# Attention and two expert layers on one core: another order of the first batch, block-diagonal products in small tiles, and a second plan table

## The chip, the cores and the metric

One core of a Trainium2 chip runs the whole program in one launch. The metric is the device time in microseconds. The kernel before takes 1292.18 us (median of 3 runs, 1291.85 to 1292.27). Engines: PE is TensorE (PEld its weight loads), DVE is VectorE, ACT is ScalarE, POOL is GpSimd, SP is SyncE, which issues most DMAs.

## What is computed

```python
# q, k, v: (8 batches, 8 heads, 576, 64); m = 32 landmarks, each the mean of 18 neighbouring rows
A  = sm(q, k_lm)         # 576 x 32: the softmax of all rows against the landmarks
Bm = sm(q_lm, k_lm)      # 32 x 32
C  = sm(q_lm, k)         # 32 x 576
Z  = Bm.T / (norm1(Bm) * norminf(Bm) + 1e-06)
for _ in range(6): Z = 2 * Z - Z @ Bm @ Z      # iterated inverse
x  = A @ Z @ C @ v                             # per head; then 4608 tokens x 512
h  = x @ w_in; x = max(0.01 * h, h) @ w_out    # 512 -> 2048 -> 512, all tokens
# then a gate picks one of 8 experts per token, and each token runs through
# relu(x @ w1[e]) @ w2[e], 512 -> 1024 -> 512, scaled by the gate's probability
```

## The kernel before

**Layout.** Batches are taken one after the other. Eight heads are two groups (g = 0, 1) of four heads; the four heads of a group stand on partitions 0–31, 32–63, 64–95 and 96–127. The attention of a batch ends in two things: `at`, the softmax A in a high and a low part, and `ub`, the product Z C v w_in, also in two parts, so that `h = at x ub` is the hidden layer. Steps run over the 16 blocks of 128 hidden units of a batch. A step ("m") issues the hidden matmuls of the block two steps ahead (`h_mm`, L545: 12 matmuls of 288 columns, four pauses) and then the output matmuls of its own block (`o_mm`, L590 for batch 0 and L595 for the others: four chunks, one for each 128 tokens, four pauses). Every second batch has four more steps ("x") for the rows over 512 tokens. After all batches come the expert steps ("e").

**Who sets the order.** Instructions are issued in the order of the program; each engine keeps that order. In each pause (a *turn*, eight in a step) the program issues what its plan table has for that time: `PLAN` holds (step position, function) of one batch's attention, begun a batch ahead, `gate_plan` those of the gate. A position of .51 falls behind the first output chunk, .88 behind the last one. In the same turns, 1.5 a turn, stands the conversion of w_in and w_out, which come as 64-bit numbers: per block two ScalarE, two VectorE and one GpSimd instruction (`conv_low`, `conv_abs`, `conv_shift`, `conv_sign`, `conv_add`), 32 blocks in all. `conv_to` forces what a step needs. The first batch's attention has no steps to stand in: the list `FIRST` issues it ahead of step 0; a bare number in it is so many conversion turns.

**Names.** `red` sums landmarks (L272); `sc` are the scores of C and Bm, `c_*`, `et`, `tv` the softmax C and its product with v; `sa` are the scores of A, `a_max` ... `a_lo` the softmax A (the *second softmax*); `b_*` is the softmax Bm; `n_g` forms I − B Bᵀ scaled, `n_k` (i = 0 to 5) is a step of the iteration, `n_y` and `n_w` bring in Bm and C v, and `u_mm` makes ub. `eight` (L279) issues matmuls of 64x32 tiles for all heads.

**A product per head** of 32 x 32 is, before, one 128x128 matmul per group: VectorE spreads the left factor over a block diagonal with a mask (`rbd`, L410, L437, L451, L458), copies or adds the rest (L452, L454, L456), and TensorE multiplies. `u0` (u_mm of batch 0) stands at the end of every even step.

PSUM: `psw` hands out two banks in turn, more in the head (`spare`), one from the expert steps on; a bank is free again when its readers are done.

Of the kernel before, what the change touches and what calls it, by code (L numbers as in the profile page):

```python
# [28 lines left out]
KA = 2  # L29
# [37 lines left out]
def kernel(  # L67
# [57 lines left out]
    m4b = C["mask4"].unsqueeze(1).unsqueeze(3).to_broadcast([128, 2, 4, LM])  # L125
# [42 lines left out]
    XE = 0.2  # L168
    XS = .4
# [216 lines left out]
    def bc4(x):  # L386
        return x.unsqueeze(2).to_broadcast([128, 2, 4, LM])
# [13 lines left out]
    def b_nrm(b):  # L401
        bl, nn = A.pop((b, "bl")), A.pop((b, "nn"))
        bb = A[b, "bb"] = small("bb", [128, 2, 2, LM])
        DVE.tensor_reduce(out=nn[:, 2:4], in_=bl, axis=AX.X, op=ALU.add)
        DVE.tensor_scalar(out=nn[:, 2:4], in0=nn[:, 2:4], scalar1=1e-9, scalar2=None, op0=ALU.add)
        DVE.reciprocal(out=nn[:, 2:4], in_=nn[:, 2:4])
        DVE.tensor_tensor(out=bb[:, 0], in0=bl, in1=bcm(nn[:, 2:4]), op=ALU.mult)
        DVE.transpose(out=bb[:, 1].rearrange("p g m -> p (g m)"), in_=bb[:, 0].rearrange("p g m -> p (g m)"))
        rb = A[b, "rb"] = small("rbd", [128, 2, 4, LM], 2)
        DVE.tensor_tensor(out=rb, in0=bc4(bb[:, 1]), in1=m4b, op=ALU.mult)  # L410

    def n_g(b):
        bb, rb = A[b, "bb"], A.pop((b, "rb"))
        ps = A[b, "gps"] = psw()
        for g in range(2):
            PE.matmul(out=ps[:, g * LM:(g + 1) * LM], lhsT=rb[:, g].rearrange("p h m -> p (h m)"),
                      rhs=bb[:, 1, g, :])
        nn = small("nn2", [128, 2, 2])
        DVE.tensor_reduce(out=nn, in_=bb, axis=AX.X, op=ALU.add)
        nbt = small("rbd", [128, 2, 4, LM], 2)  # L420
# [10 lines left out]
        DVE.tensor_tensor(out=gs, in0=ps[:, :2 * LM].rearrange("p (g m) -> p g m", g=2),  # L431
                          in1=bcm(cc), op=ALU.mult)
# [3 lines left out]
        rb = A[b, "rb"] = small("rbd", [128, 2, 4, LM], 2)  # L436
        DVE.tensor_tensor(out=rb, in0=bc4(rx[:, :, 0, :]), in1=m4b, op=ALU.mult)  # L437
        DVE.tensor_tensor(out=rx[:, :, 1, :], in0=rx[:, :, 0, :], in1=eye, op=ALU.add)

    def n_k(b, i):  # L440
        rx, rb = A[b, "rx"], A[b, "rb"]
        lo, hi = {0: (0, 1), 5: (1, 2)}.get(i, (0, 2))
        ps = psw()
        for g in range(2):
            PE.matmul(out=ps[:, 64 * g + LM * lo:64 * g + LM * hi], lhsT=rb[:, g].rearrange("p h m -> p (h m)"),  # L445
                      rhs=rx[:, g, lo:hi, :])
        p4 = ps[:, :128].rearrange("p (g a m) -> p g a m", g=2, a=2)
# [34 lines left out]
    def u_mm(b, s, n=2):  # L482
# [15 lines left out]

    PLAN = [
# [8 lines left out]
        (8.25, a_exp, 0), (8.3, a_max, 1), (8.4, a_sub, 1), (8.63, n_k, 1), (8.8, a_sum, 0), (8.9, a_exp, 1),
        (9.0, a_mul, 0), (9.26, n_k, 2), (9.4, a_sum, 1), (9.5, a_mul, 1), (9.88, n_k, 3), (10.05, a_tr, 0),
        (10.2, a_hi, 0), (10.3, a_lo, 0), (10.51, n_k, 4), (10.7, a_tr, 1), (10.85, a_hi, 1), (10.95, a_lo, 1),  # L510
        (11.13, n_k, 5), (11.15, wi_load, 0), (11.3, wi_load, 1), (11.63, n_y), (12.13, n_w), (12.63, u_mm, 0),
        (13.88, u_mm, 2), (15.13, u_mm, 4), (18.13, u_mm, 6),
# [531 lines left out]

    grp = ExitStack()
# [64 lines left out]
    for s in range(NSLOT):  # L1110
        t0 = T1 + NF * s
        x = t0 - 1 - XE - 5 * XS
        if s == 0:
            p = t_early + 0.4
        else:
            p = max(t_rest + 0.5 if s == KA else 0, x - 2.5)
        if s == 1:
            p = max(p, T1 - 2)
            x = max(x, p + 1)
        put([(p, part(s_tab, s))])  # L1120
        put([(p + 0.6 if j < XGB else x + XS * (j - XGB) + 0.1, part(s_gather, s, j)) for j in range(5)])
        put([(x + XS * j, part(s_xt, s, j)) for j in range(5)])
# [4 lines left out]
    def first_h(_, t):  # L1127
# [45 lines left out]
    for t in range(TE + 1):  # L1173
# [42 lines left out]
        if t < NFC and t % 2 == 0 and t // 2 + 2 < NS:  # L1216
            u0(t // 2 + 2)
# [74 lines left out]
```

## Time and profile before

| | us |
|---|---|
| median of 3 runs | 1292.18 |
| profiled execution | 1291.29 |
| its span | 1289.5 |
| TensorE busy | 1227.5 (95%) |
| VectorE, ScalarE, GpSimd busy | 609.0, 512.9, 468.8 |
| mean granted clock of TensorE | 0.988 of full speed |

The page's digits show VectorE at 5 to 8 tenths in the first five slices of 32 us and at 3 to 5 after; TensorE at 5, 7, 8, 8 tenths in the first four slices and at 9 or more from the fifth to the last but one. In a timeline a row merges equal instructions that follow each other; its second number runs from the first start to the last end, and since matmuls overlap, a group's share of TensorE is read from its start to the next group's start. A matmul in 32-bit floats stands as two instructions, so "x4" are two matmuls.

### The profile page before, as it was taken

The numbers are of one execution on the slowest core, as the hardware profiler recorded it, in microseconds if no ns is written. First come the engines' busy times: TensorE is split into PE (matmuls) and PEld (weight loads), VectorE is DVE, ScalarE is ACT, GpSimd is POOL, SyncE is SP. The second block draws the span as 40 slices with busy tenths as digits, with TensorE's granted clock in tenths as the row PEclk, the third lists the DMA queues.
The fourth block names the chain that finished last, engine by engine and source line by source line (L and its number), as shares of the span: only waits on it lengthen the run. The fifth ranks groups of instructions, "written<-read, shape, count | busy, mean of one in ns | idle before, by whom it ended". The sixth has DMA issues, their size and how long they took to land.

```text
span 1289.5 us, 22321 instructions
## 1 busy us (share of the span) xinstructions
PE 1227.5 (95%) x8630; PEld 1006.5 (78%) x8630; DVE 609.0 (47%) x1546; ACT 512.9 (40%) x1117; POOL 468.8 (36%) x362
## 2 busy tenths in 40 slices
PE   5788999999999999999999999999999999999994
PEld 2545567877877887878887888789989999999993
DVE  7788566535455435465435443244353332333311
ACT  3455355444344343344343444542343343333211
POOL 1544324433423424423424334624353333333201
PEclk9989999999999999999999999999999999999997
DMA  7677462351151241151141122341454334433001
GB/s 254 232 246 238 147 233 60 115 166 53 34 190 52 66 166 52 36 188 52 67 165 52 41 92 90 120 139 34 156 175 157 122 103 140 131 120 109 21 31 39
DMA packets 61891, 151.04 MB, mean 117 GB/s; under 512 B 10192, under 2 KB 19664, under 8 KB 61776
## 3 DMA queue, kind: packets, MB, share of 16 engines
q1 hardware_dynamic: 54736, 130.61, 30.8%
q0 software_dynamic: 7040, 18.92, 4.5%
q8 instruction: 70, 1.15, 0.4%
q14 instruction: 45, 0.37, 0.1%
HBM read 121.87 MB, written 27.63 MB: 116 GB/s over the span
## 4 chain that ended last, share of the span: by engine, by line
PE 79%; DVE 9%; issue 4%; ACT 1%; DMA 0%; POOL 0%; POOLq 0%; SPq 0%; DVEq 0%; ACTq 0%
PE acc L595 34%; PE hps L899 14%; PE hps L545 14%; PE psw L279 3%; PE acc L604 3%; PE psw L921 2%; PE acc L590 2%; PE psw L445 1%; PE psw L867 1%; PE psw L634 1%; DVE kT L272 1%; DVE qlm L272 1%; PE psw L378 1%; DVE te L199 1%; PE psw L642 1%
## 5 line engine op out<-in xcount | busy, mean ns | idle before, releaser
L595 PE MATMUL acc<-wo,gh 128*128 128x512 f32 x1216 | 383.8, 397 | 0.0
L562 POOL TENSOR_TENSOR gl<-hs,gh 128x512 fp32r<-128x512 f32 x112 | 147.1, 1313 | 311.5 <-ACT gh L561 183.2
L595 PEld LDWEIGHTS acc<-wo,gh 128*128 128x128 f32 x1216 | 217.6, 188 | 48.2 <-issue 11.7
L545 PE MATMUL hps<-at,ub 128*128 128x288 f32 x1536 | 253.4, 307 | 1.6 <-DVE hs L551 1.5
L545 PEld LDWEIGHTS hps<-at,ub 128*128 128x128 f32 x1536 | 220.9, 191 | 33.7 <-issue 20.0
L595 PE MATMUL acc<-wo,gl 128*128 128x512 f32 x608 | 238.0, 391 | 0.0
L551 DVE TENSOR_TENSOR hs<-hps,hs 128x288 f32<-128x288 f32 x224 | 98.9, 451 | 130.0 <-ACT hs L549 129.8
L908 DVE SCALAR_TENSOR_TENSOR gl<-hps,gh 128x288 fp32r<-128x288 f32 (+1 forms) x128 | 54.0, 423 | 197.3 <-ACT gh L904 197.3
L595 PEld LDWEIGHTS acc<-wo,gl 128*128 128x128 f32 x608 | 114.2, 188 | 25.0
L549 ACT ACTIVATE hs<-hps 128x288 f32<-128x288 f32 x256 | 101.9, 414 | 74.3 <-PE hps L545 71.1
L904 ACT ACTIVATE gh<-hps 128x288 fp32r<-128x288 f32 x128 | 52.8, 412 | 176.1 <-PE hps L899 111.6
L561 ACT CAST gh<-hs 128x512 fp32r<-128x512 f32 x112 | 69.5, 620 | 119.0 <-PE acc L595 94.4
L855 POOL DMA_INDIRECT xg<-x_d,gi x40 | 41.6, 1041 | 132.4 <-DVE gi L847 61.1
L940 POOL DMA_INDIRECT out_dram<-rows,gi x40 | 40.6, 1015 | 124.8 <-DVE rows L938 75.8
L492 DVE TENSOR_TENSOR ub<-psw,ub 128x512 fp32r<-128x512 f32 (+1 forms) x70 | 41.3, 632 | 70.0 <-ACT ub L491 70.0
L899 PE MATMUL hps<-xt,wo 128*128 128x288 f32 x480 | 68.7, 297 | 0.0
L899 PE MATMUL hps<-at,wo 128*128 128x288 f32 x480 | 68.0, 296 | 0.0
L899 PEld LDWEIGHTS hps<-xt,wo 128*128 128x128 f32 x480 | 66.4, 188 | 1.6
L899 PEld LDWEIGHTS hps<-at,wo 128*128 128x128 f32 x480 | 65.8, 188 | 1.6
L491 ACT CAST ub<-psw 128x512 fp32r<-128x512 f32 (+1 forms) x70 | 34.6, 547 | 65.6 <-PE psw L279 65.6
L595 PE MATMUL acc<-ub,gh 128*128 128x512 f32 x192 | 59.8, 393 | 0.0
L887 POOL TENSOR_TENSOR wo<-wraw,wo 128x1024 fp32r<-128x1024 f32 x20 | 48.0, 2398 | 23.3 <-ACT wo L883 23.0
(244 smaller groups left out, 1805.0 us busy)
## 6 DMA issues: line engine op xcount, KB each, us to landing
wraw<-in_moe_w_dram SPq DMA_DIRECT2D x64, 512.0 KB, 4.1
wi<-wi_d SPq DMA_DIRECT2D x56, 512.0 KB, 4.5
kT<-in_k_dram SPq DMA_DIRECT2D x32, 288.0 KB, 5.1
qT<-in_q_dram SPq DMA_DIRECT2D x32, 288.0 KB, 5.3
raw<-in_moe_w_in_dram SPq DMA_DIRECT2D x16, 512.0 KB, 5.2
vraw<-in_v_dram SPq DMA_DIRECT2D x16, 512.0 KB, 5.4
raw<-in_moe_w_out_dram SPq DMA_DIRECT2D x16, 512.0 KB, 4.6
x_d<-rows SPq DMA_DIRECT2D x32, 256.0 KB, 3.3
```

Of the source, the lines that this page charges most:

```text
L492: DVE.tensor_sub(out=u[:, :, 1, :], in0=p3, in1=u[:, :, 0, :].bitcast(F32))
L545: PE.matmul(out=ps[:, :HT], lhsT=us[:, wl, c:c + 128], rhs=at[:, al, 2 * (b % 2) + g, c0:c1], start=(n == 0), stop=(n == 5))
L549: ACT.mul(out=hs[:, c0:c1], in_=ps[:, :HT], mul=0.01)
L551: DVE.tensor_max(out=dst[:, c0:m], in0=ps[:, :m - c0], in1=hs[:, c0:m])
L561: ACT.copy(out=gh[:, :512], in_=src)
L562: POOL.tensor_tensor(out=gl, in0=src, in1=gh[:, :512].bitcast(F32), op=ALU.subtract)
L595: PE.matmul(out=acc(key, j), lhsT=g[hl][:, j * 128:(j + 1) * 128], rhs=wsel[:, wl, :], start=(f == 0 and i == 0), stop=(f == nf - 1 and i ...
L855: POOL.indirect_dma_start(out=xg[:n, :], out_offset=None, in_=x2_d[0:rows, :], in_offset=IND(ap=M[s, "gi"][:n, 0, j:j + 1], axis=0), bound ...
L887: (POOL if n % 2 else DVE).tensor_tensor(out=r[:, :, 1], in0=raw.rearrange("p (f c) -> p f c", f=2), in1=r[:, :, 0].bitcast(F32), op=ALU.s ...
L899: PE.matmul(out=ps[:, :HT], lhsT=wr[:, wl, d * 128:(d + 1) * 128], rhs=xt[:, al, d, c0:c1], start=(n == 0), stop=(n == 11))
L904: ACT.activation(out=gh[:, c0:c1], in_=ps[:, :HT], func=AF.Relu)
L908: DVE.scalar_tensor_tensor(out=lo, in0=ps[:, a - c0:b - c0], scalar=0.0, in1=gh[:, a:b].bitcast(F32), op0=ALU.max, op1=ALU.subtract)
```

## The change

- `diag` is new: a product per head is four matmuls of 32x32 tiles on the diagonal. `n_g`, `n_k` and `n_y` use it; the spread copies `rbd` go. An `n_k` adds its old value with a second set of `diag` products against the identity, into the same bank, and one ScalarE copy hands the result to the next `n_k`, where three VectorE instructions did.
- `FIRST` has another order: the second softmax (`sa`, `a_max`, ...) stands ahead of and between the iteration, 21 conversion turns instead of 30. The first batch's scores of A lie in `hs`.
- `u0` of batch 0 moves from the end of an even step to position .51 of the odd step behind it.
- `PLAN` has other positions, mostly .51 and .88, and batch 1 has a table of its own, `PLAN_1`. `gate_plan` moves the gate's later parts behind. The transposes of the expert steps (`s_xt`) get other positions.

```diff
-                A[b, "st", g] = wide("st")[:, :S]
+                A[b, "st", g] = (wide("st")[:, :S] if b else gp.tile([128, S], F32, name="hs", tag="hs", bufs=2))
...
+    def diag(out, lhs, rhs, start=True, stop=True):
+
+        for p in range(4):
+            h = slice(32 * p, 32 * p + 32)
+            PE.matmul(out=out[h], lhsT=lhs[h], rhs=rhs[h], start=start, stop=stop, skip_group_check=True)
...
-        rb = A[b, "rb"] = small("rbd", [128, 2, 4, LM], 2)
-        DVE.tensor_tensor(out=rb, in0=bc4(bb[:, 1]), in1=m4b, op=ALU.mult)
...
     def n_k(b, i):
-        rx, rb = A[b, "rx"], A[b, "rb"]
+
+        rx = A[b, "rx"]
         lo, hi = {0: (0, 1), 5: (1, 2)}.get(i, (0, 2))
         ps = psw()
         for g in range(2):
-            PE.matmul(out=ps[:, 64 * g + LM * lo:64 * g + LM * hi], lhsT=rb[:, g].rearrange("p h m -> p (h m)"),
-                      rhs=rx[:, g, lo:hi, :])
...
-        if i < 5:
-            DVE.tensor_tensor(out=nb, in0=bc4(p4[:, :, 0, :]), in1=m4b, op=ALU.mult)
-            DVE.tensor_copy(out=nx[:, :, 0, :], in_=p4[:, :, 0, :])
-        if i > 0:
-            DVE.tensor_tensor(out=nx[:, :, 1, :], in0=p4[:, :, 1, :], in1=rx[:, :, 1, :], op=ALU.add)
...
+            c, m, e = 64 * g + LM * lo, 64 * g + LM, 64 * g + 2 * LM
+            diag(ps[:, c:c + LM * (hi - lo)], rx[:, g, 0, :], rx[:, g, lo:hi, :], stop=hi == 1)
+            diag(ps[:, m:e], C["eye"], rx[:, g, 1, :], start=hi == 1)
+        nx = A[b, "rx"] = small("rx", [128, 2, 2, LM], 2)
+        ACT.copy(out=nx[:, :, lo:, :], in_=ps[:, :128].rearrange("p (g a m) -> p g a m", g=2, a=2)[:, :, lo:, :])
...
-        (3.625, sc, 1), (4.125, sc, 0), (4.0, b_max), (4.3, c_max, 0), (4.5, c_max, 1), (4.52, b_exp),
+        (3.88, sc, 1), (4.2, b_max), (4.4, b_exp), (4.88, sc, 0), (5.05, c_max, 0), (5.15, c_exp, 0), (5.2, c_max, 1),
...
+        (2.88, sc, 1), (3.2, b_max), (3.4, b_exp), (4.51, sc, 0), (4.7, c_max, 0), (4.8, c_exp, 0), (4.9, c_max, 1),
...
-        P += [(t, g_l2), (t + 0.1, g_l3), (2.88 + NX * (b % 2), g_l4), (3.4 + NX * (b % 2), g_sc)]
+        P += [(t, g_l2), (t + 0.1, g_l3), (3.51 + NX * (b % 2), g_l4), (4.0 + NX * (b % 2), g_sc)]
...
+    put([(2 * i - 2.49, part(u0, i)) for i in range(2, NS)])
...
-        x = t0 - 1 - XE - 5 * XS
+        xp = [t0 + x for x in (-3.45, -3.08, -2.45, -2.08, -1.45)]
...
-        (c_max, 0), (b_nrm,), (c_exp, 0), (n_g,), (c_max, 1), 6, (et, 0, 0), (c_exp, 1), (et, 0, 1), 4,
-        (n_k, 0), (c_rec, 0), (tv, 0), (et, 1, 0), 4, (et, 1, 1), (n_k, 1), (v_load, 1), (sa, 0), (sa, 1), 2,
+        (sa, 0), 2, (c_max, 0), (b_nrm,), (c_exp, 0), (n_g,), (sa, 1), (a_max, 0), (a_sub, 0), (c_max, 1),
+        (et, 0, 0), (et, 0, 1), (c_exp, 1), (a_max, 1), (a_sub, 1), (n_k, 0), (a_exp, 0), (c_rec, 0), (tv, 0),
...
-        if t < NFC and t % 2 == 0 and t // 2 + 2 < NS:
-            u0(t // 2 + 2)
```

Three places in the order of the engines. First VectorE in the head of before, between the second and the third `n_k` (`te` are conversions, `rbd` and `rx` the iteration, `tn` and `csm` the softmax C):

```order
L452 COPY rx<-acc_237 128x2x32
L456 COPY rx<-rx 128x2x32
L355 TENSOR_SCALAR csm<-csm 128x1
L356 RECIPROCAL csm<-csm 128x1
L383 TENSOR_SCALAR tn<-acc_247,csm 128x64
L199 TENSOR_SCALAR te<-te 128x512
L203 SCALAR_TENSOR_TENSOR te<-raw,te 128x512
L451 TENSOR_TENSOR rbd<-psw_287,cst 128x256
L452 COPY rx<-psw_287 128x2x32
L454 TENSOR_TENSOR rx<-psw_287,rx 128x2x32
```

In the changed kernel the hand-over stands on ScalarE (`raw` and `te` are conversions, `hs` the exponential of the second softmax, `et` copies of the softmax C):

```order
L348 ACTIVATE sc,csm<-sc,csm 128x576
L445 COPY rx<-psw_257 128x128
L303 ACTIVATE hs<-hs 128x576
L445 COPY rx<-hps 128x128
L192 ACTIVATE raw<-raw 128x512
L188 ACTIVATE te<-raw 128x512
L363 COPY et<-acc_332 128x512
L366 COPY et<-acc_338 64x128
L445 COPY rx<-acc_346 128x128
```

The iteration's results moved from VectorE to ScalarE, where they stand between exponentials, conversions and copies.

Second, VectorE in a steady batch of before, ahead of `sc` 1 (`pay`, `grk`, `gpf`, `gpi` are the gate's last part, `kT` and `qlm` the landmark sums, the last of which `sc` 1 waits for):

```order
L272 TENSOR_REDUCE qlm<-qT 128x32
L702 TENSOR_REDUCE pay<-gex 128x5
L703 TENSOR_SCALAR pay<-pay 128x5
L704 RECIPROCAL pay<-pay 128x5
L705 TENSOR_SCALAR pay<-cst 128x5
L706 TENSOR_TENSOR grk<-psw_5254,cst 128x40
L708 TENSOR_TENSOR grk<-grk,oh 128x40
L709 TENSOR_REDUCE gpf<-grk 128x5
L710 CAST gpi<-gpf 128x5
L272 TENSOR_REDUCE kT<-kT 128x32
L551 TENSOR_TENSOR hs<-hps,hs 128x288
L272 TENSOR_REDUCE qlm<-qT 128x32
```

And the same place of the changed kernel:

```order
L269 TENSOR_REDUCE kT<-kT 128x32
L553 TENSOR_TENSOR hs<-hps,hs 128x288
L269 TENSOR_REDUCE qlm<-qT 128x32
L553 TENSOR_TENSOR hs<-hps,hs 128x288
L704 TENSOR_REDUCE pay<-gex 128x5
L705 TENSOR_SCALAR pay<-pay 128x5
L706 RECIPROCAL pay<-pay 128x5
L707 TENSOR_SCALAR pay<-cst 128x5
L708 TENSOR_TENSOR grk<-psw_5658,cst 128x40
L710 TENSOR_TENSOR grk<-grk,oh 128x40
L711 TENSOR_REDUCE gpf<-grk 128x5
L712 CAST gpi<-gpf 128x5
```

The gate's eight instructions moved from ahead of the last two landmark sums to behind them.

Third, TensorE around one full `n_k` of batch 2 before:

```order
L595 MATMUL acc_1690<-wo_2173,gl 128x512
L445 MATMUL psw_2434<-rx,rbd 128x64 x2
L595 MATMUL acc_1696<-wo_2173,gh 128x512 x2
L595 MATMUL acc_1696<-wo_2173,gl 128x512
L595 MATMUL acc_1705<-wo_2173,gh 128x512 x2
```

And in the changed kernel:

```order
L597 MATMUL acc_1827<-wo_2297,gl 128x512
L387 MATMUL psw_2607<-rx 32x64 x4
L387 MATMUL psw_2607<-rx,cst 32x32 x4
L387 MATMUL psw_2607<-rx 32x64 x4
L387 MATMUL psw_2607<-rx,cst 32x32 x4
L597 MATMUL acc_1846<-wo_2297,gh 128x512 x2
```

Two matmuls over the whole array became sixteen over 32x32 tiles, at the same kind of place behind the first output chunk.

## Rows read from the trace of the kernel before

**Rows 1.** Busy time by stage: stretch, length, then each engine's busy us; PEclk.
```profile
53.95:173.15 119.20, 108.48 (x713) 62.53 (x711) 86.57 (x195) 58.38 (x129) 45.66 (x35) 0.96 0.68 223
289.50:764.00 474.50, 470.29 (x3779) 380.47 (x3778) 239.03 (x669) 200.99 (x499) 173.67 (x141) 1.00 0.27 89
```

**Rows 2.** Timeline of TensorE in the head: start us, us, engine line op.
```profile
16.78 1.06 PE L416 MATMUL psw<-bb,rbd 128*128 128x32 f32 x4 [2.99 <-DVE rbd L410]
...
44.60 1.11 PE L279 MATMUL acc<-wi,wt 64*32 64x256 f32 x16 [0.47 <-DVE wt L480]
...
46.49 7.62 PE L545 MATMUL hps<-at,ub 128*128 128x288 f32 x36
```

**Rows 3.** Timeline of the other engines in the head.
```profile
21.36 0.24 ACT L369 COPY et<-hps 64x128 f32<-64x128 f32 x1
...
27.57 0.48 DVE L290 STREAM_TRANSPOSE st<-psw 128x288 f32<-128x288 f32 x1 [0.19 <-PE hps L279]
...
41.23 1.40 POOL L326 TENSOR_TENSOR at<-s,at 128x576 fp32r<-128x576 f32 x1 [2.80 <-ACT at L322]
...
49.02 1.30 POOL L216 TENSOR_TENSOR wi<-raw,te 128x512 uint32<-128x512 uint32 x1
```

**Rows 4.** Timeline of TensorE in steps 4 to 7: the two longest waits.
```profile
89.68 1.12 PE L365 MATMUL psw<-cst,sc 128*128 128x128 f32 x4 [3.48 <-DVE ub L492]
...
107.43 0.93 PE L279 MATMUL psw<-wi,wt 64*32 64x256 f32 x16 [2.52 <-DVE st L290]
```

**Rows 5.** Groups of VectorE: line, operation, count | busy us, mean ns.
```profile
L451 DVE TENSOR_TENSOR rbd<-psw,cst 128x256 f32<-128x256 f32 x37 | 15.5, 419 | 11.8 <-PE psw L445 11.8
...
L456 DVE COPY rx<-rx 128x64 f32<-128x64 f32 x8 | 2.4, 299 | 0.0
```

**Rows 6.** The chain that ended last: one step's four output chunks of batch 0.
```profile
154.93 3.43 PE acc L590 x8
```

**Rows 7.** Timeline of TensorE: `sc` 1 of two batches.
```profile
487.98 0.76 PE L279 MATMUL psw<-kT,qlm 64*32 64x320 f32 x12
489.32 0.73 PE L279 MATMUL psw<-kT,qlm 64*32 64x320 f32 x4 [0.58 <-DVE qlm L272]
...
577.93 0.76 PE L279 MATMUL psw<-kT,qlm 64*32 64x320 f32 x12
579.92 0.73 PE L279 MATMUL psw<-kT,qlm 64*32 64x320 f32 x4 [1.23 <-DVE qlm L272]
```

**Rows 8.** Timeline of VectorE: the gate's last part, and the sum behind it.
```profile
485.15 0.19 DVE L702 TENSOR_REDUCE pay<-gex 128x5 f32<-128x40 f32 x1
...
487.50 0.75 DVE L272 TENSOR_REDUCE kT<-kT 128x32 f32<-128x576 f32 x1
```

**Rows 9.** Timeline of TensorE: one full `n_k` between output chunks.
```profile
518.33 0.55 PE L445 MATMUL psw<-rx,rbd 128*128 128x64 f32 x4
518.69 0.71 PE L595 MATMUL acc<-wo,gh 128*128 128x512 f32 x2
```

**Rows 10.** Timeline of TensorE: blocks in small tiles, and output matmuls around one.
```profile
500.95 0.90 PE L378 MATMUL psw<-vraw,et 128*32 128x64 f32 x40
...
506.49 0.62 PE L595 MATMUL acc<-wo,gh 128*128 128x512 f32 x2
506.94 0.39 PE L595 MATMUL acc<-wo,gl 128*128 128x512 f32 x1
507.26 0.71 PE L279 MATMUL psw<-qT,kT 64*32 64x288 f32 x16
507.91 0.73 PE L595 MATMUL acc<-wo,gh 128*128 128x512 f32 x2
...
539.05 1.09 PE L279 MATMUL psw<-wi,wt 64*32 64x256 f32 x32
```

**Rows 11.** Timeline of ScalarE and of TensorE at the end of the attention.
```profile
827.35 1.99 ACT L883 CAST wo<-wraw 128x1024 fp32r<-128x1024 f32 x2
...
831.13 0.66 PE L634 MATMUL psw<-cst,rows 128*128 128x128 f32 x4 [2.04 <-DVE xt L870]
```

More of the change, by code (lines that the diff above doesn't have):

```diff
@@ L408, in b_nrm @@
         DVE.transpose(out=bb[:, 1].rearrange("p g m -> p (g m)"), in_=bb[:, 0].rearrange("p g m -> p (g m)"))
[L409 to L410 removed]
     def n_g(b):
[L413 to L414 removed]
+        bb = A[b, "bb"]
+        ps = psw()
         for g in range(2):
[L416 to L417 removed]
+            diag(ps[:, 64 * g:64 * g + LM], bb[:, 1, g, :], bb[:, 1, g, :])
         nn = small("nn2", [128, 2, 2])
         DVE.tensor_reduce(out=nn, in_=bb, axis=AX.X, op=ALU.add)
[L420 removed]
+        nbt = small("nbt", [128, 2, 4, LM])
         nb, nt = nbt[:, 0], nbt[:, 1]
@@ L430, in n_g @@
         gs = small("bl", [128, 2, LM])
[L431 removed]
+        DVE.tensor_tensor(out=gs, in0=ps[:, :128].rearrange("p (g m) -> p g m", g=2)[:, :, :LM],
                           in1=bcm(cc), op=ALU.mult)
@@ L508 @@
[L508 to L512, printed above, removed]
+        (3.88, sc, 1), (4.2, b_max), (4.4, b_exp), (4.88, sc, 0), (5.05, c_max, 0), (5.15, c_exp, 0), (5.2, c_max, 1),
@@ new lines @@
+        (5.3, b_nrm), (5.4, c_exp, 1), (5.6, c_rec, 0), (5.88, et, 0, 0), (5.89, et, 0, 1),
+        (6.51, tv, 0), (6.52, et, 1, 0), (6.55, v_load, 1), (6.7, c_rec, 1), (6.88, et, 1, 1), (6.89, n_g),
+        (7.51, sa, 0), (8.51, sa, 1), (8.7, a_max, 0), (8.75, a_sub, 0), (8.88, tv, 1), (8.89, n_k, 0),
+        (9.1, a_exp, 0), (9.15, a_max, 1), (9.25, a_sub, 1), (9.51, n_k, 1), (9.6, a_sum, 0), (9.7, a_exp, 1),
+        (9.8, a_mul, 0), (9.88, n_k, 2), (10.1, a_sum, 1), (10.2, a_mul, 1), (10.51, n_k, 3), (10.6, a_tr, 0),
@@ new lines @@
+        (10.88, n_k, 4), (10.9, a_hi, 0), (11.0, a_lo, 0), (11.15, wi_load, 0), (11.2, a_tr, 1), (11.3, wi_load, 1),
+        (11.51, n_k, 5), (11.6, a_hi, 1), (11.7, a_lo, 1), (11.88, n_y), (12.51, n_w), (12.88, u_mm, 0),
+        (13.88, u_mm, 2), (14.88, u_mm, 4), (18.51, u_mm, 6),
+    ]
+    PLAN_1 = [
+        (0.05, qk_load, 'k', 0), (0.1, qk_load, 'q', 0), (0.15, qk_load, 'k', 1), (0.2, qk_load, 'q', 1),
+        (0.3, qk_load, 'k', 2), (0.4, qk_load, 'q', 2), (0.5, qk_load, 'k', 3), (0.6, qk_load, 'q', 3),
+        (0.7, red, 'k', 0), (0.9, red, 'q', 0), (1.0, v_load, 0), (1.15, red, 'k', 1), (1.4, red, 'q', 1),
+        (1.65, red, 'k', 2), (1.9, red, 'q', 2), (2.15, red, 'k', 3), (2.4, red, 'q', 3),
+        (2.88, sc, 1), (3.2, b_max), (3.4, b_exp), (4.51, sc, 0), (4.7, c_max, 0), (4.8, c_exp, 0), (4.9, c_max, 1),
+        (5.1, b_nrm), (5.2, c_exp, 1), (5.4, c_rec, 0), (5.88, et, 0, 0), (5.89, et, 0, 1),
+        (6.51, tv, 0), (6.52, et, 1, 0), (6.55, v_load, 1), (6.7, c_rec, 1), (6.88, et, 1, 1), (6.89, n_g),
+        (7.88, sa, 0), (8.51, sa, 1), (8.7, a_max, 0), (8.75, a_sub, 0), (8.88, tv, 1), (8.89, n_k, 0),
+        (9.1, a_exp, 0), (9.15, a_max, 1), (9.25, a_sub, 1), (9.6, a_sum, 0), (9.7, a_exp, 1), (9.8, a_mul, 0),
+        (9.88, n_k, 1), (10.1, a_sum, 1), (10.2, a_mul, 1), (10.51, n_k, 2), (10.6, a_tr, 0), (10.88, n_k, 3),
+        (10.9, a_hi, 0), (11.0, a_lo, 0), (11.15, wi_load, 0), (11.2, a_tr, 1), (11.3, wi_load, 1),
+        (11.6, a_hi, 1), (11.7, a_lo, 1), (11.88, n_k, 4), (12.3, n_k, 5), (12.51, n_y), (12.88, n_w),
+        (13.51, u_mm, 0), (14.51, u_mm, 2), (15.51, u_mm, 4), (18.51, u_mm, 6),
@@ L523, in attn_plan @@
         return [(start(b - 1) + pos if pos < NFC else start(b) + pos - NFC, part(fn, b, *a))
-                for pos, fn, *a in PLAN]
+                for pos, fn, *a in (PLAN_1 if b == 1 else PLAN)]
     G = {}
@@ L1115 @@
         else:
-            p = max(t_rest + 0.5 if s == KA else 0, x - 2.5)
+            p = max(t_rest + 0.5 if s == KA else 0, xp[0] - 2.5)
         if s == 1:
             p = max(p, T1 - 2)
-            x = max(x, p + 1)
+            xp = [max(x, p + 1 + i / 100) for i, x in enumerate(xp)]
         put([(p, part(s_tab, s))])
-        put([(p + 0.6 if j < XGB else x + XS * (j - XGB) + 0.1, part(s_gather, s, j)) for j in range(5)])
-        put([(x + XS * j, part(s_xt, s, j)) for j in range(5)])
+        put([(p + 0.6 if j < XGB else xp[j - XGB] + 0.1, part(s_gather, s, j)) for j in range(5)])
+        put([(xp[j], part(s_xt, s, j)) for j in range(5)])
     def first_u0(_, s):
```

45 lines of the change are left out of this document (12 added, 33 removed).

## The prediction

> **What bounds the kernel now.** I read the busy time by stage first, then TensorE's timeline in each stage, then VectorE's and ScalarE's where TensorE waits. The reader is to see three stages. From 289.5 to 764 us, most of the steady run of batches 2 to 7, TensorE is busy 470.3 of 474.5 us [rows 1]: every instruction put on TensorE there makes the kernel longer, and beside that only a wait of TensorE is worth removing. Before 46.5 us TensorE follows the first batch's attention, with VectorE between its groups [rows 2, 3]. In steps 0 to 15 (53.95 to 173.15 us) it is busy 108.5 of 119.2 us, so 10.7 are idle, and its mean granted clock is 0.96, which loses 0.04 x 119.2 = 4.8 more [rows 1]. The two longest waits there, 3.48 + 2.52 = 6.0 us, end on VectorE [rows 4].
>
> The sum is made against the profiled execution: 1291.29 us, of which the span is 1289.5; the median of the runs is 1292.18, 0.9 us more.
>
> **A. The head up to the first hidden-layer matmul.** Before, that matmul starts at 46.49 us, 29.7 us behind the n_g matmuls of 16.78 [rows 2]. In the new order the first half of the second softmax's scores stands ahead of n_g: a score half, two transposes of 0.48 [rows 3] and a maximum come before the normalisation, while a masked copy goes, so n_g starts about 1.2 us later, and n_k 0, behind another score half and five transposes, near 21.7 us. From there VectorE is out of the iteration. One n_k is then a TensorE group of about 1.0 us (n_g's four instructions took 1.06 [rows 2]), a ScalarE copy of 0.25 (0.24 for 64x128 [rows 3]) and two hand-overs of 0.1, 1.45 in all, 8.7 for six. In between stand one tv of some 1.4, one et of 1.3, and on ScalarE an exponential that ends near 24.1 and two conversion pairs: n_k 5 ends near 32.6, n_y near 33.4, n_w near 35, and u_mm 0 starts near 35.3 instead of 44.60 [rows 2], 9.3 earlier. The stage does not end there: u_mm 1 needs the fourth converted block, and GpSimd reaches it late. The low half of the last attention rows, 1.40, can start near 35.4, and two conversion additions of 1.30 stand behind it [rows 3]: 39.4, with some stretching 40. The two u_mm took 1.89 (44.60 to 46.49), so one takes 0.95, and the first hidden matmul starts near 41. I take −5.5. Bounds: −9.3 if those additions come early, 0 if ScalarE's conversions stand ahead of the copies as VectorE's did. Nine fewer conversion turns stand in the head (21 for 30); seven of them are forced before step 0 ends its first part, under 36 hidden matmuls, which hide them.
>
> **B. Steps 0 to 15.** VectorE loses seven groups of instructions, in all 48.2 us over eight batches; the largest and the smallest are shown [rows 5]. That is 6.0 us less for batch 1. ScalarE gets six copies of 0.25, 1.5 us. Batch 1's reductions and first scores come up to a step earlier, and a u_mm of the first batch stands alone in each odd step. I let the waits for VectorE shrink by the 6.0 us of work that goes, and the loss of clock that follows such waits by 3.5 of its 4.8: −9.5. Against it stand 1.4 us for batch 1's iteration on TensorE (D): −8.1, say −8. What is late next is u_mm: its result has three o_mm chunks until its reader, three quarters of 3.43 us [rows 6], 2.6 us, where it had a whole step. Bounds: −14 (all 15.5 of idle time and clock, less 1.4), and +4 if each of six u_mm holds its reader 0.7 us longer than TensorE waits now.
>
> **C. The scores of batches 2 to 7.** sc 1 stands after the second o_mm chunk of step 3, and its last four instructions wait for the last reduction: 489.32 against 487.98, and 579.92 against 577.93 [rows 7]. Delays of 1.34 and 1.99 alternate by the batch's parity, six in all: 3 x 1.34 + 3 x 1.99 = 10.0. On VectorE eight gate instructions stand ahead of the last two reductions, from 485.15 to 487.50 [rows 8]. The new plan puts the gate (3.51) behind them and sc 1 two chunks later (3.88): the reductions are done 2.3 us earlier and asked for 1.4 us later, 3.7 against delays of up to 2.0. I take −10.0; the upper bound is −6, if 0.7 stays in each.
>
> **D. The iteration on TensorE, batches 2 to 7.** Before, an n_k is four 128x128 instructions: 0.36 us to the next start, and the o_mm pair behind it takes 0.71 [rows 9] where an undisturbed pair takes 0.62 [rows 10]: 0.45 in all. Now it is sixteen 32x32 matmuls, four rounds of four, each matmul two instructions. What a block in small tiles costs is read from two: sixteen instructions of 288 columns, two rounds, take 0.71 us, thirty-two of 256 columns, four rounds, 1.09 [rows 10]. The difference, 0.38 us over 1024 − 576 columns, is 0.85 ns a column. Of the 0.65 us from 507.26 to the next start that leaves 0.16; with 0.09 ahead of the block (506.94 to 507.26 is 0.32, undisturbed starts are 0.23 apart) and 0.11 behind it (0.73 for 0.62), a block costs 0.35 beside its columns [rows 10]. No row shows four row groups, so the rounds are bounded: 54 ns for 64 columns, 27 to 54 for 32. A full n_k is 4 x 54 + 4 x (27 to 54) = 0.33 to 0.43, with 0.35 some 0.73: +0.28. n_k 5, eight short rounds, +0.23; n_k 0 the same, less the 0.26 of entry and exit that it shares with tv, −0.03; n_g and n_y, four short rounds, +0.06 each. Per batch 4 x 0.28 + 0.32 = 1.44 (0.9 to 2.0); six batches +8.6 (5.4 to 11.8). ScalarE's copy is due three chunks or more later, so no wait is added. The Trainium skill says that changing the tiling mode drains TensorE (TensorEngine Tiling (Array Packing), Tiling Modes); the trace agrees, with those 0.09 us, which n_k did not pay before.
>
> **E. The end of the attention.** At 831.13 TensorE has waited 2.04 us for a bank; ScalarE did two weight casts from 827.35 on, 1.99 us, ahead of the copy that frees it [rows 11]. That transpose now stands a chunk earlier, ahead of those casts. The wait should fall to about 0.5: −1.5, and with some clock behind it −2 (−4 to +1, since three transposes now stand in one place).
>
> **Sum.** −5.5 − 8 − 10 + 8.6 − 2 = −16.9; 1291.3 − 16.9 + 0.9 = 1275. The likeliest case's own range is 1267 to 1284.
>
> **Rivals.**
> *Four row groups take turns (slower).* The sixteen matmuls of an n_k write one bank. If they go one after the other, a full n_k streams 16 x 54 + 16 x (27 to 54) ns, 1.3 to 1.7 us instead of 0.33 to 0.43, and a batch costs 7 to 9 us more instead of 1.4; over seven batches 49 to 63 instead of 10, so 1314 to 1328, say 1320. It decides from 3.9 us a batch on, where the other terms (25.5, and 1.4 in B) are used up. For it: every row group in this trace writes a bank of its own. Against it: tv's forty instructions of 64 columns, in four column groups of one bank, take 0.90 us [rows 10] where 40 x 54 ns would be 2.2; here too each tile has partitions of its own. The Trainium skill states that different row tiles cannot access the same PSUM bank simultaneously (TensorEngine Tiling (Array Packing), Restrictions and Gotchas); no run here shows it, and by that rule the time is this rival's.
> *VectorE stays late.* For it: at 89.68 its subtraction came 3.48 us late [rows 4], and u_mm's reader is now half a step away, so the wait moves there. Against it: 6 us less work. A and B give nothing, and 1.4 is added: −10 + 8.6 − 2 + 1.4 = −2, 1290.
> *ScalarE holds the iteration.* Conversions, exponentials and copies share one queue; then the second softmax is beside the iteration in name only, and A is 0: 1281. Against it: between the six copies stand only two conversion pairs.
> *All of it goes.* A −8, B −13, D +6: 1265.
>
> **How the numbers follow.** Forecast 0.62, row groups in turn 0.10, VectorE late 0.10, ScalarE 0.10, all of it 0.08. The range 1263 to 1291 leaves out the first rival and the tails. A measurement tells about 0.2%, 2.6 us, from no change, so "same" is 1289.6 to 1294.8: faster 0.62 + 0.10 + 0.08 and half of the VectorE rival, 0.85; same 0.05; slower 0.10.
>
> **What would show it.** A: the first hidden matmul near 41 us, and n_k after n_k with only a copy between them. B: no wait over 2 us between 48 and 160 us and a clock near 1.00. C: the sixteen instructions of sc 1 start together. D: 0.7 us from n_k's first start to the next group's; 1.5 or more means the first rival. E: no wait of 2 us before the last steps. A first hidden matmul later than 46, a u_mm reader that waits over 2 us, or n_k above 1.2 us make the prediction wrong.

## The result, and the profile after

The changed kernel takes 1275.31 us (median of 4 runs, 1274.8 to 1276.42) beside 1292.22 for the kernel before: a ratio of 0.9865, 95% interval 0.9848 to 0.9883. The forecast was 1275. The profiled execution took 1276.42 us with a span of 1274.6, 14.9 less than before: it is the longest of its four, and that of before, 1291.29, lies below every timed run of before, so the traces show 2 us less gain than the medians.

Busy time by stage after the change. Columns as in [rows 1]; the two stretches answer to the two there (steps 0 to 15, and 474.5 us of the steady run):

```profile
49.98:156.90 106.92, 103.17 (x894) 56.92 (x895) 87.17 (x178) 59.96 (x133) 47.16 (x36) 1.00 0.77 255
274.50:749.00 474.50, 470.82 (x4713) 366.67 (x4698) 219.38 (x567) 204.19 (x524) 171.76 (x140) 1.00 0.27 89
```

Steps 0 to 15 are 12.3 us shorter. TensorE is idle 3.75 us there instead of 10.7, and its clock is 1.00 instead of 0.96. The steady run looks as busy as before, which hides that the same work now takes longer there.

To see that, I follow three starts of TensorE through the traces: the first hidden matmul, the `x_mm` of batch 1 and the `x_mm` of batch 7. They cut the span into the head, the first batches, and the attention of batches 3 to 7. Four kernels stand in the table, two of them experiments told below:

| us | head, to first hidden matmul | to `x_mm` of batch 1 | to `x_mm` of batch 7 | span |
|---|---|---|---|---|
| before | 46.49 | 215.94 | 560.19 | 1289.5 |
| tiles alone | 41.30 | 215.84 | 567.84 | 1291.5 |
| order alone | 47.05 | 208.55 | 559.45 | 1278.7 |
| both: the change | 41.27 | 206.14 | 563.65 | 1274.6 |

The head gained 5.2, the first batches 9.8; the run of batches 3 to 7 lost 3.5. From the last hidden matmul of the attention to the first of the experts it is 23.21 us for 25.54, a gain of 2.3; from there to the end 448.7 us for 449.7, a gain of 1.0.

The third column has a spread of its own: four more kernels below, with the same plan for these batches as the change, took 561.2 to 563.6 us (experiments 7, 9, 10 and 12), where the same waits come out longer or shorter (5.1 us in all in the change, 3.2 in experiment 9). So causes in that stretch are read from waits by name, not from its length alone.

The head, on TensorE's timeline (start us, us, engine line op), answers to [rows 2]:

```profile
35.35 1.11 PE L276 MATMUL acc<-wi,wt 64*32 64x256 f32 x16 [0.48 <-DVE wt L464]
38.83 1.08 PE L276 MATMUL psw<-wi,wt 64*32 64x256 f32 x8 [2.37 <-POOL wi L213]
40.26 1.08 PE L276 MATMUL psw<-wi,wt 64*32 64x256 f32 x8 [0.35 <-POOL wi L213]
41.27 7.62 PE L547 MATMUL hps<-at,ub 128*128 128x288 f32 x36
```

`u_mm` 0 starts 9.25 us earlier, and `u_mm` 1 then waits for GpSimd's conversions, as the working of A had it.

The same timeline in the steady run: `sc` 1, which answers to [rows 7], and a full `n_k`, which answers to [rows 9]. The sixteen score instructions now start in one run; the `n_k` takes 0.48 us from its first start to the next group's.

```profile
475.38 0.77 PE L276 MATMUL psw<-kT,qlm 64*32 64x320 f32 x16
...
507.43 0.39 PE L597 MATMUL acc<-wo,gl 128*128 128x512 f32 x1
507.75 0.31 PE L387 MATMUL psw<-rx 32*32 32x64 f32 x8
507.88 0.24 PE L387 MATMUL psw<-rx,cst 32*32 32x32 f32 x8
507.94 0.29 PE L387 MATMUL psw<-rx 32*32 32x64 f32 x8
508.06 0.24 PE L387 MATMUL psw<-rx,cst 32*32 32x32 f32 x8
508.23 0.73 PE L597 MATMUL acc<-wo,gh 128*128 128x512 f32 x2
```

What TensorE still waits for: the longest wait of steps 4 to 7, which answers to [rows 4], and then the waits from batch 1's `x_mm` to batch 7's (waiter and what released it: us in total, times, longest):

```profile
87.52 0.66 PE L362 MATMUL psw<-cst,sc 128*128 128x128 f32 x4 [2.21 <-DVE ub L476]
```

```profile
PE hps L547 <- DVE csm L352: 2.1, 3, 0.7
PE hps L547 <- DVE hs L553: 1.5, 1, 1.5
PE psw L276 <- DMA wi<-wi_d: 1.4, 2, 0.7
```

The 1.5 us were there before. The two other lines are new, and no term of the prediction had them: a hidden matmul that waits for VectorE in batches 3, 5 and 7, and `u_mm` waiting for its weights' DMA. At the end of the attention the longest wait left is one of an expert transpose for ScalarE, where 2.04 us stood before [rows 11]:

```profile
819.76 0.66 PE L869 MATMUL psw<-cst,xg 128*128 128x128 f32 x4 [0.61 <-ACT xt L637]
```

### The profile page after: what moved, and what is told of

It is laid out like the page before. It is cut to its first block, busy times and chain, and to the rows that moved or that the text cites. A ratio compares the mean times of both kernels' runs of the same rounds, so it can differ in the third digit from the quotient of the medians.

```text
span 1274.6 us, 25205 instructions
## 1 busy us (share of the span) xinstructions
PE 1224.5 (96%) x10166; PEld 981.4 (77%) x10166; DVE 583.0 (46%) x1394; ACT 522.0 (41%) x1165; POOL 472.1 (37%) x362
## 4 chain that ended last, share of the span: by engine, by line
PE 82%; DVE 6%; issue 5%; DMA 2%; ACT 1%; POOL 0%; ACTq 0%; POOLq 0%
PE acc L597 35%; PE hps L547 15%; PE hps L901 14%; PE psw L276 4%; PE acc L606 3%; PE acc L592 2%; PE psw L923 2%; DMA wi<-wi_d 2%; PE psw L387 2%; PE psw L869 1%; PE psw L636 1%; DVE te L196 1%; PE psw L375 1%; DVE te L200 1%; PE psw L644 1%
## 5 line engine op out<-in xcount | busy, mean ns | idle before, releaser
L547 PE MATMUL hps<-at,ub 128*128 128x288 f32 x1536 | 239.9, 304 | 4.7 <-DVE csm L352 2.3
L547 PEld LDWEIGHTS hps<-at,ub 128*128 128x128 f32 x1536 | 212.3, 189 | 30.9 <-issue 17.1
L889 POOL TENSOR_TENSOR wo<-wraw,wo 128x1024 fp32r<-128x1024 f32 x20 | 51.1, 2557 | 31.2 <-ACT wo L885 30.9
```

The source lines that it names most:

```text
L547: PE.matmul(out=ps[:, :HT], lhsT=us[:, wl, c:c + 128], rhs=at[:, al, 2 * (b % 2) + g, c0:c1], start=(n == 0), stop=(n == 5))
L889: (POOL if n % 2 else DVE).tensor_tensor(out=r[:, :, 1], in0=raw.rearrange("p (f c) -> p f c", f=2), in1=r[:, :, 0].bitcast(F32), op=ALU.s ...
```

## Experiments

The runs were made on several chips, on which the kernel before took 1290.1 to 1292.2 us, so kernels are compared by ratio to it, or by the stretches of their traces.

**1 and 2. The tiles alone, the order alone.** The first is the kernel before with `diag` and the changed `b_nrm`, `n_g`, `n_k`, `n_y`; the second is the changed kernel with those functions as before. In short, for both:

```diff
 (kernel before)                       (kernel after)
-def bc4 / masked copies in n_*        -def diag
+def diag, n_* in 32x32 tiles          +def bc4 / masked copies in n_*
```

> The kernel before with the diagonal tiles alone (diag, and b_nrm, n_g, n_k, n_y as changed), all places as before. Theory: TensorE pays 1.0 us a batch from batch 2 and about that in batch 1 (+7), the eight sc waits stay (they hang on VectorE's reductions), and the waits for the four-fold copies go in the head and in steps 0 to 15 (the four that the trace of before puts down to rbd: 8.6 us in all, some of it given to other waits): 1287 to 1295. Rival: the gain of the change is VectorE's relief, wherever the work stands: 1282 or less.

> The changed kernel with the iteration as before (four-fold copies on VectorE, whole 128-row matmuls): the new order alone. Theory: TensorE saves the 7 us of the tiles, the sc waits stay gone, and VectorE's extra work (0.5 us or more an iteration step) comes back as waits where the plan is dense, the head and steps 0 to 15, 7 us or more: 1273 to 1283, and no better than the change. Rival: the order does all of it: 1268 or less.

Measured: tiles alone 1293.83 us, ratio 1.0011 (1.0001 to 1.0022); order alone 1282.29, ratio 0.9922 (0.9903 to 0.9941). Both theories hold in the total, and the table above says where each acts; not in the place, since the tiles alone give 0.1 us in the first batches, where the first theory saw part of its gain. The head is the tiles' work alone: 41.30 with the old list. The first batches are the order's: 7.4 us without the tiles, 9.8 with them, while the tiles without the order give 0.1. In the steady run the tiles cost 7.65 us without the order, and the order alone gives 0.7, far less than the 7.8 that its score blocks save (24.83 to 17.05 us for the twenty score blocks there); new waits take most of the rest, above all that of experiment 4 (1.3 us in each of three batches there). Of the tiles' 7.65 us, D's blocks explain some 5.

**3. A later `u_mm` 2.**

```diff
-(13.88, u_mm, 2), (14.88, u_mm, 4)
+(14.51, u_mm, 2), (15.88, u_mm, 4)
```

> The changed kernel with two numbers of the plan for batches 2 to 7 other: u_mm 2 at 14.51 instead of 13.88, u_mm 4 at 15.88 instead of 14.88. Theory: the second u_mm of a batch stands one step behind the first (before: 1.25 steps), and its half of the input weights lands 0.7 to 0.9 us late; with more room the blocks that last 2.0 to 2.2 us fall to 1.22, five of them, so 3 us: 1272.3. Rival: the load is started by the u_mm in front of it and SyncE's queue, so a later u_mm 2 only moves the wait to u_mm 4, and the time stays at 1275.3.

Measured: 1272.63 us, ratio 0.9854 (0.9839 to 0.9869). The waits for the DMA are gone. What a block costs is counted here from the matmul ahead of it to behind the pair that follows it, less what those matmuls take undisturbed: so counted, the twenty-one blocks of `u_mm` from batch 1's `x_mm` to batch 7's cost 25.66 us for 27.91, and 25.65 before the change. The stretch is 2.5 us shorter. The total alone would not show it, for its interval overlaps the change's; but every kernel here with the change's places of `u_mm` has such a wait in that stretch, 0.2 to 1.4 us in all, and none with the later places. One block of `u_mm`, first in the changed kernel, then in this one; what was cut in two by a wait runs through:

```profile
428.99 0.66 PE L276 MATMUL psw<-wi,wt 64*32 64x256 f32 x16
430.40 0.67 PE L276 MATMUL psw<-wi,wt 64*32 64x256 f32 x16 [0.75 <-DMA wi<-wi_d]
```

```profile
430.08 1.09 PE L276 MATMUL psw<-wi,wt 64*32 64x256 f32 x32
```

**4. A later `b_nrm`, and 5. `b_nrm` without L405.** Experiment 5 leaves out the addition of 1e-9 to a sum of exponentials of which one is 1.

```diff
-(5.3, b_nrm), (5.4, c_exp, 1), (5.6, c_rec, 0),
+(5.4, c_exp, 1), (5.6, c_rec, 0), (5.61, b_nrm),
```
```diff
-DVE.tensor_scalar(out=nn[:, 2:4], in0=nn[:, 2:4], scalar1=1e-9, scalar2=None, op0=ALU.add)
```

> The changed kernel with b_nrm of batches 2 to 7 at 5.61, behind c_rec, instead of 5.3. Theory: VectorE's 128x2 addition of L405 stood 1.9 us in batches 3, 5 and 7 because it began while GpSimd worked, and ended within 0.04 us of GpSimd's TENSOR_TENSOR; the accumulation behind it came late, and TensorE stood 0.95 us in each of the three. Half a turn later GpSimd is idle: L405 takes 0.17 us, and 2.9 us go: 1272.4. Rival: another instruction of VectorE takes the wait in its place (c_rec's L352 starts in the same stretch), and the time stays at 1275.3.

> The changed kernel without L405, the addition of 1e-9 to a sum of exponentials. Theory: what holds VectorE is that its operands come through what GpSimd uses at that moment, so the next instruction of that kind, L407 with two operands, stands the 1.7 us instead, TensorE's 0.95 us stays, and the time stays within 0.5 us of 1274.6 (the span). Rival: the stretch belongs to L405's form alone, and its going takes 2.9 us: a span near 1271.7.

Measured: with the later `b_nrm` 1272.07 us, ratio 0.985 (0.9835 to 0.9865), again not clear of the change's interval; without L405 1274.22 in a single run, a span of 1272.3 on a chip where the kernel before was 1.5 us faster, so that figure alone decides nothing. The timelines show why. In the changed kernel an addition of two numbers a partition takes 1.91 us. It begins 0.41 us into an instruction of GpSimd's scatter of the gate (`g_sc`, which the change moved too, from 3.4 to 4.0), stands through the rest of it and through the TENSOR_TENSOR behind it, and ends at 293.16, 0.03 after that; the hidden matmul behind it waits:

```profile
290.84 0.97 POOL L722 DMA_INDIRECT tab_d<-pay,gpi  x1 [0.31 <-issue]
...
291.25 1.91 DVE L405 TENSOR_SCALAR nn<-nn 128x2 f32<-128x2 f32 x1
...
291.83 1.30 POOL L564 TENSOR_TENSOR gl<-hs,gh 128x512 fp32r<-128x512 f32 x1
...
294.30 1.06 PE L547 MATMUL hps<-at,ub 128*128 128x288 f32 x6 [0.70 <-DVE csm L352]
```

Without L405 the product behind it (L406 in that kernel's numbers) stands instead, to 292.45, 0.10 after GpSimd's end:

```profile
290.40 0.17 DVE L405 RECIPROCAL nn<-nn 128x2 f32<-128x2 f32 x1
290.61 1.84 DVE L406 TENSOR_TENSOR bb<-bl,nn 128x64 f32<-128x64 f32 x1
...
291.05 1.30 POOL L563 TENSOR_TENSOR gl<-hs,gh 128x512 fp32r<-128x512 f32 x1
```

So the stall changes its owner, as the theory had it, but TensorE's share of it halves, 0.86 to 0.45 us in each of the three batches (counted from start to start; the theory had it stay): behind the held product only the transpose is left, while behind L405 a reciprocal and the product had to follow first. The kernels of experiments 9 and 10 show the same with L405 in place: in these three batches it began 0.24 to 0.27 us into the scatter's instruction and took 0.17 us, the product behind it stood 1.71 to 1.73 us, and TensorE waited 0.3. So the halving does not need L405 to go, only another moment. With the later `b_nrm` L405 still ends with GpSimd, but loses 0.3 us instead of 1.7, and no matmul waits:

```profile
291.41 0.14 DVE L352 TENSOR_SCALAR csm<-csm 128x1 f32<-128x1 f32 x1
...
291.90 0.46 DVE L405 TENSOR_SCALAR nn<-nn 128x2 f32<-128x2 f32 x1
...
291.01 1.31 POOL L564 TENSOR_TENSOR gl<-hs,gh 128x512 fp32r<-128x512 f32 x1
...
291.77 1.84 PE L547 MATMUL hps<-at,ub 128*128 128x288 f32 x12
```

**6. Both places later**, `u_mm` and `b_nrm`, the two edits above together.

> Both edits of the two kernels beside it. Theory: two waits that don't touch each other, 3 + 2.9 us: 1269.4. Rival: one cover for the other (the batch's weight loads shift with the stretch), so the sum is that of one: 1272.

Measured: 1269.35 us, ratio 0.9827 (0.9814 to 0.9841), the first clear of the change's interval. From batch 1's `x_mm` to batch 7's it takes 558.70 us, 4.95 less than the change and 1.5 less than before. TensorE's idle time in the steady 474.5 us goes from 3.7 to 0.1:

```profile
272.40:746.90 474.50, 474.38 (x4775) 370.62 (x4760) 218.50 (x580) 207.81 (x530) 172.89 (x141) 1.00 0.27 89
```

**7. The old head in the changed kernel, and 8. in the kernel with both later places.**

```diff
-FIRST = [..., (sa, 0), 2, (c_max, 0), (b_nrm,), (c_exp, 0), (n_g,), (sa, 1), ...
+FIRST = [..., (c_max, 0), (b_nrm,), (c_exp, 0), (n_g,), (c_max, 1), 6, ...  (list of before)
```

> The changed kernel with the FIRST list of before, and its second softmax in the wide tile as before. Theory: the head is on the path alone; the first hidden matmul falls back to between 44 and 46.5 us (the iteration now on ScalarE's side keeps some of the gain), all behind it keeps its length: 1278.5 to 1280.5. Rival: the iteration in small tiles is what makes the head short, and the list does nothing: 1275 to 1276.

> Both later places (b_nrm, u_mm of batches 2 to 7) with the head's list of before. Theory: the list of the head gives nothing, since with the tiles alone the first hidden matmul starts at 41.3 already; the time is that of both edits, 0.9827 of before, within 0.0005. Rival: the old list is better by 1 to 2 us, as the single run of each on one chip looked (1274.06 against 1276.04 for the changed list with n_k's matmuls in another order): 0.9815.

Measured: 1274.06 us, ratio 0.9855 (0.9833 to 0.9877), and 1267.74, ratio 0.9826 (0.9813 to 0.9839). In the first the theory fell: the first hidden matmul stays at 41.77 us, so the list does next to nothing. In the second its theory holds: both lists are equal. TensorE's timeline in two more heads: the old list with the tiles (experiment 1), then the new list without them (experiment 2).

```profile
39.41 1.11 PE L279 MATMUL acc<-wi,wt 64*32 64x256 f32 x16 [0.48 <-DVE wt L467]
40.23 1.14 PE L279 MATMUL psw<-wi,wt 64*32 64x256 f32 x16
41.30 2.53 PE L532 MATMUL hps<-at,ub 128*128 128x288 f32 x12
```

```profile
41.13 1.11 PE L277 MATMUL acc<-wi,wt 64*32 64x256 f32 x16 [0.47 <-DVE wt L478]
44.60 1.08 PE L277 MATMUL psw<-wi,wt 64*32 64x256 f32 x8 [2.37 <-POOL wi L214]
46.03 1.08 PE L277 MATMUL psw<-wi,wt 64*32 64x256 f32 x8 [0.35 <-POOL wi L214]
47.05 7.62 PE L561 MATMUL hps<-at,ub 128*128 128x288 f32 x36
```

With the new list `u_mm` 1 waits 2.37 + 0.35 us, with the tiles and without them, for conversions on GpSimd; with the old one they are done, and `u_mm` 0 is 4.1 us later instead. Both ways end at 41.3.

**9. One plan for all batches, and 10. the first batch's `u_mm` where it was.**

```diff
-for pos, fn, *a in (PLAN_1 if b == 1 else PLAN)
+for pos, fn, *a in PLAN
```
```diff
-put([(2 * i - 2.49, part(u0, i)) for i in range(2, NS)])
+if t < NFC and t % 2 == 0 and t // 2 + 2 < NS: u0(t // 2 + 2)   (behind step t)
```

> The changed kernel with the plan of batches 2 to 7 for batch 1 too. The new order as a whole shortens the stretch from the first hidden matmul to batch 1's x steps by 7.4 us with the old iteration and by 9.8 with the tiles. Theory: half or more of it is batch 1's own plan, whose reductions and scores come up to a step earlier: 1278.5 to 1281. Rival: it is the place of u_mm in the odd steps, and this plan does nothing: 1274.5 to 1276.

> The changed kernel with the first batch's u_mm behind every even step, as before, instead of inside the odd steps. Theory: they share the stretch's 9.8 us with the plan, and 2 to 5 us come back as waits of the hidden matmuls for the subtraction: 1277.5 to 1280. Rival: their new place costs as much as it gives, since the one wait over 2 us left in this stretch (2.4 us at 84.72 us) ends on such a subtraction: 1273 to 1276.

Measured: 1279.35 us, ratio 0.992 (0.9904 to 0.9935), and 1279.33, ratio 0.9912 (0.9897 to 0.9927). The stretch from the first hidden matmul to batch 1's `x_mm` is 211.2 us in both, 5.1 longer than the change's. Each undoes half of the order's gain, so it needs both. The longest waits that come back are one for a transpose of the scores with one plan, and one for GpSimd's conversion with the old place; waits for other VectorE work come back beside them. The places of the gate, of the scores and of the expert transposes were not put back one by one, so C and E rest on their traces.

```profile
103.12 1.02 PE L276 MATMUL psw<-wi,wt 64*32 64x256 f32 x16 [2.91 <-DVE st L287]
```

```profile
57.84 0.64 PE L276 MATMUL psw<-wi,wt 64*32 64x256 f32 x8 [3.15 <-POOL wi L213]
```

**11. The last long wait of the first batches.** Both later places, and in batch 1's plan:

```diff
-(5.88, et, 0, 0), (5.89, et, 0, 1), (6.51, tv, 0), (6.52, et, 1, 0), ... (6.88, et, 1, 1), (6.89, n_g),
+(6.26, et, 0, 0), (6.27, et, 0, 1), (6.76, tv, 0), (6.77, et, 1, 0), ... (7.13, et, 1, 1), (7.14, n_g),
```

The two rows left out between them, `v_load` 1 and `c_rec` 1, move by 0.25 and 0.15 too.

> Both later places (b_nrm, u_mm of batches 2 to 7), and in batch 1's plan the transposes of the first softmax at 6.26 instead of 5.88, with tv and n_g up to 0.25 step later. Theory: the wait of 2.4 us for a bank at 84.72 us goes, since the subtraction that frees it is done by then: 2.0 to 2.4 us under the kernel with both edits (0.9827 of before), 0.981. Rival: VectorE is what is late in this stretch, and the wait comes back at the next group: 0.9827.

Measured: 1270.41 us, ratio 0.9845 (0.9831 to 0.9858): no gain, and 1.5 us lost up to batch 1's `x_mm` by the traces. The rival is right, and more: the wait stays as long and only has another owner, the hidden matmul that reads the late subtraction, and TensorE's clock falls behind it.

```profile
86.73 1.65 PE L547 MATMUL hps<-at,ub 128*128 128x288 f32 x8 [2.10 <-DVE ub L476]
```

Its granted clock (next to the last columns, DMA share and GB/s) goes to the lower level of 1.2 GHz; with the `et` at its earlier place (experiment 6), behind a wait of 2.2 us at the same spot, it stays at 1.00 throughout:

```profile
86.00:88.00 2.00, 1.27 (x8) 0.88 0.90 271
88.00:90.00 2.00, 2.00 (x11) 0.50 0.83 207
90.00:92.00 2.00, 2.00 (x5) 0.76 1.11 291
```

Part of VectorE's lateness there is again a hold by GpSimd. In the changed kernel, ahead of the subtraction that ends the wait, a conversion instruction of VectorE takes 1.53 us beside GpSimd's addition and ends 0.55 us behind it; 1.5 us earlier, with no instruction of GpSimd beside it, the same instruction took 0.65 us. No run here takes it away.

```profile
84.61 1.54 POOL L213 TENSOR_TENSOR wi<-raw,te 128x512 uint32<-128x512 uint32 x1 [2.25 <-ACT hs L551]
...
85.17 1.53 DVE L200 SCALAR_TENSOR_TENSOR te<-raw,te 128x512 uint32<-128x512 uint32 x1
```

**12. `n_k` row group by row group.** In the queue both matmuls of one row group now stand together, then those of the next.

```diff
-diag(ps[:, c:c + LM * (hi - lo)], rx, ...); diag(ps[:, m:e], eye, ...)
+for p in range(4): PE.matmul(ps[h, c:...], rx[h], ...); PE.matmul(ps[h, m:e], eye[h], ...)
```

> The changed kernel with n_k's matmuls in another order: both of one row group behind each other, then the next group's, instead of all four groups in turn. Theory: four row groups work beside each other only as they follow in the queue, and a group's second matmul waits for its first: a full n_k goes from 0.67 us to 0.9 to 1.0 over the plain rate, 7 to 10 us in all: a span of 1281 to 1285. Rival: the groups take turns in any case, or all overlap in any order: the span stays within 1 us of 1274.6.

Measured: 1276.04 us in a single run, a span of 1274.3. The theory fell, the rival (any order overlaps) holds: a full `n_k`, counted as in experiment 3, costs 0.71 us where it was 0.67. The trace even shows the starts out of the queue's order, the first matmuls (L444) of all four groups ahead of the second ones (L446):

```profile
507.54 0.33 PE L444 MATMUL psw<-rx 32*32 32x64 f32 x8
507.68 0.25 PE L446 MATMUL psw<-rx,cst 32*32 32x32 f32 x7
507.74 0.22 PE L444 MATMUL psw<-rx 32*32 32x64 f32 x1
```

## Why the prediction was right, and where it was not

The total was right to a microsecond by the medians, and that is luck: between the traces the gain is 14.9 us for 16.9, and the parts missed by more. B and D came out 3.0 and 2.5 us better than forecast and the experts' steps, priced at nothing, 1.0 better; a part of 7.9 us that no term had stood against them. The mechanisms of C, D and E held; A's gain had another source than the order, and B's another than the work taken off VectorE.

**A, the head:** −5.2 for −5.5. The size and the mechanism behind it held (`u_mm` 0 at 35.35 us, forecast 35.3; GpSimd's additions end the stage). Its credit was wrong: the working began with the new order, and the runs give all of it to the iteration in tiles and off VectorE; the list adds nothing.

**B, steps 0 to 15:** from the first hidden matmul to the end of step 15, −11.0 for −8. The stage itself is 12.3 shorter: the idle time fell by 7.0 (6.0 were allowed), and all 4.8 of lost clock came back (3.5 were allowed). Against that, the time from the first hidden to the first output matmul grew by 1.2 us, from 7.46 to 8.70, on a conversion of GpSimd. "No wait over 2 us" failed at one place, 2.21 us at 87.52, on the subtraction of the rival "VectorE stays late" (the waiter needs its bank, and does not read `ub`); experiment 11 says that this wait belongs to VectorE and not to its waiter. That 6.0 us less work on VectorE would do it was wrong as a cause: that relief alone gives 0.1 here (experiment 1). Batch 1's plan and the place of `u_mm` are each worth 5 us, and the relief 2.4 on top.

**C, the scores:** −7.7 us in five batches, by the same rate −9.3 for six where −10.0 was forecast. The mechanism held.

**D, the iteration:** +5.05 us in five batches, by the same rate 6.1 for six where 8.6 was forecast, inside the bounds. An `n_k` is 0.48 us from its first start to the next group's, where 0.7 was to be seen; that 0.7 was a slip, for the working's own 0.73 holds 0.09 ahead of the block and 0.11 behind it, which leaves 0.53. It costs 0.67 us in all for the 0.73 of the working, 0.45 before: +0.22 for +0.28, since the short rounds came out near their lower bound. `n_k` 5 is +0.13 for +0.23. ScalarE's copy held nobody up in the steady run.

**What was missing:** C and D together should have given −1.4 us; from the end of step 15 to the last hidden matmul the change lost 4.7 instead (641.16 to 645.84 us). The step that failed is the one that priced the other moves of the plan at nothing. `u_mm` 2 stands 1.0 step behind `u_mm` 0 where it had 1.25, and its weights come late: 2.3 us in five batches. `b_nrm` came beside instructions of GpSimd that it had not met, and its stall reaches a hidden matmul: 3 x 0.86 = 2.6. Experiments 3, 4 and 6 remove them. Batch 2's attention, in the steps before batch 1's `x_mm`, lost 1.2 more, where C and D at their rate should have saved 0.5. About 1.2 us of the 560 behind it I can put down to no row; it is still there with both places later.

**E, the end:** −2.3 for −2; no wait of 2 us is left there. Two of the expert transposes wait for ScalarE, 0.24 and 0.61 us, near the 0.5 of the forecast.

Of the rivals, "four row groups take turns" is refuted: 0.48 us from start to start, not 1.3 or more. Where the Trainium skill says that different row tiles cannot access the same PSUM bank at the same time (TensorEngine Tiling (Array Packing), Restrictions and Gotchas), the measurement decides: four diagonal row groups, each with partitions of its own in one bank, ran side by side here. "ScalarE holds the iteration" did not cost the head its gain, though its copies do come late there: TensorE waits for them four times, 1.67 us at 23.58, where the copy stands behind an exponential, and 0.4 to 0.8 us after that; the stage still ends on GpSimd. The version with both places later, at 0.9827 of the time before, beats both kernels; with the old head it is the same.

## What to carry to other kernels

Price every row of a plan that moves, also those whose instructions stay the same: ask which load it now follows more closely, and which engine works beside it at its new time. Try two parts of a change apart before giving either the credit; here the tiles alone were no gain, the order alone a little over half of it, and they needed each other. A wait that ends on a late engine changes its owner when the waiter is moved, so move the work ahead of it on that engine.

## What the runs showed of the hardware

A VectorE instruction can stand until GpSimd's instruction has ended, and through the next one too: L405 (one operand, two numbers a partition) took 1.91 us instead of 0.17, and ended 0.03 us after GpSimd's; with it gone, a product of two operands stood 1.84 us the same way. Not all of GpSimd's time holds it: an L405 that began 0.24 to 0.27 us into the scatter's instruction took 0.17 us (experiments 9 and 10). A one-number instruction of the same kind (L352) was not held: 0.14 us at 291.41 in experiment 4, inside the 1.31 us of GpSimd's. The Trainium skill describes a pair of ports that VectorE and GpSimd lock for a whole instruction, taken by VectorE in its two-port modes or with two operands in SBUF (SBUF — State Buffer, SBUF: two separate sides); the trace agrees with one operand, here of two numbers a partition, and with two operands.

Row groups of TensorE do not wait for each other in the queue's order (experiment 12: 0.71 us for 0.67, with starts out of that order), so "each engine keeps that order" of the kernel's description does not hold between them. And two waits of 2.1 and 2.2 us at the same place were followed by different clocks: by the lower level in one kernel (0.88, 0.50 and 0.76 in three slices of 2 us), by no change in the other; why, no run here settles.
